# A gated attention and feed-forward kernel on one core: last batch's units moved, two blocks' turns exchanged, Down products made transposed

## The chip, the core and the metric

The kernel runs on one NeuronCore of one Trainium2 chip. The metric is device time in microseconds; the kernel before has a median of 1188.56 us over 12 runs (1186.95 to 1189.96). PE is TensorE (matmuls), PEld its weight load, DVE is VectorE, ACT is ScalarE, POOL is GpSimd and SP is SyncE, which here only issues DMAs. `Lnnn` is a line of the kernel before.

## The reference

```python
scores = (1.0 / S) * np.matmul(z, z.transpose(0, 2, 1))   # z: 8 x 3008 x 64
attn = np.maximum(scores, 0.0) ** 2
x = (u * np.matmul(attn, v)).reshape(B * S, D)            # u, v: 8 x 3008 x 256
h = x @ w_in                                              # 256 x 2048
g = h * (1.0 / (1.0 + np.exp(-1.702 * h)))
out = g @ w_out                                           # 2048 x 256, float32 out
```

Scores are symmetric, so a block of squared scores can be computed once and turned for the other triangle.

## The kernel before

**Chunks.** Each batch's 3008 rows are cut into six chunks of 512 (the last 448); rows are also counted in 24 blocks of 128, the last of which has 64 rows and is stored twice, in both halves of the partitions. A *unit* (i, jp) is a pair of row blocks of scores against chunk i: PE makes the scores (L235), ACT applies Relu into a tile `rl` (L256), DVE squares it into a tile `a` (L270, L261). Units on or above the diagonal only are computed; those of other chunks are turned by a DMA transpose from SP into tiles `tt` (`turn_unit`, L298), halves of a diagonal pair into `ad` (L263), and the last chunk's own unit into `al` (L277).

**Attention.** `attend` runs over the 24 row blocks of V as weights with squared scores moving (L358), the sum over blocks in PSUM; most matmuls use half of the array's rows in pairs. In batches after the first, chunk i reads its own first blocks, then those behind the diagonal, then turned blocks of earlier chunks, and at the end the three blocks of the last chunk, which come from `tt` too. `gate` (L375) multiplies with `u`, which arrives in column groups of 32 and is turned by a 32 x 32 transpose on DVE (L202). Scores of later units are put between the attention's steps by tables: `SCHED` says before which step of which chunk how many units are taken from the queue. `SCHED_LAST` is the table of the last batch. The first two units of a batch that are still missing are taken behind the last product of the batch before.

**Feed-forward.** `up_group` (L399) multiplies with W1 for two of 16 blocks of 128 features, ACT applies Gelu (L407), and a second pass, on DVE (L411) or on ACT (L409) for some groups, scales into `gt`. The Down projection pairs neighbouring row blocks, columns and feature halves in a seven-product scheme (P1 to P7, Winograd's form of Strassen): `left_sum` forms S1 to S4 on DVE (L467 to L476), `weight_sums` four sums of W2 once. Each product is 8 matmuls per pair of row blocks; P6, P7 and P4 add to P1's bank, P3 to P5's. Between them ACT copies banks out and DVE adds (L530, L532, L536). Batches come in twos: the two halves of the last row block of an even and an odd batch are joined, so an even batch's last block has 384 rows (one pair and an `odd` block, L493), an odd one's 512.

**Order.** The order of all instructions on each engine is the program's order, with a manual schedule: there is no planner. From group 16 on, an up group and a product alternate; ten or so products remain at the end of a batch, and with the last one the store of the last block. Stores (`store`, L562) go out on SP, with the last 64 rows of two batches on POOL; in the last batch's last block `store_part` (L551 to L556) issues quarters on SP and ACT. All DMAs of SP go out in order, and each also waits for the one issued eight DMAs earlier. `y` tiles have two buffers; they share these with the `zst` tiles of the next z.

**First batch.** Its squared blocks are turned in the order of the list `ORDER0`, each pair as soon as both units are there and all earlier entries are done.

Of the kernel before, what the change touches and what calls it, by code (L numbers as in the profile page):

```python
# [9 lines left out]
F32 = mybir.dt.float32  # L10
F16 = mybir.dt.float16
P = 128
# [3 lines left out]
def kernel(  # L16
# [13 lines left out]
    AF = mybir.ActivationFunctionType  # L30
    ALU = mybir.AluOpType

    B, S, D = u.shape
# [26 lines left out]
    W2 = const.tile([P, NFF, D], F16, name="W2")  # L60
    WT = const.tile([P, 4, NFF // 2, P], F16, name="WT")
# [180 lines left out]
    def square(b, i, jp, sc):  # L242
# [35 lines left out]
        if jp // 2 > i and (turned(b, i) or jp < NU - 2):  # L278
            if b and i == 0 and LATE:
                late.append(((jp + 2) % NU, lambda: turn_unit(b, i, jp, a)))  # L280
            elif b == 0 and jp < NU - 2:
                squared.setdefault((i, jp // 2), []).append(lambda: turn_unit(b, i, jp, a))
                while ORDER0 and len(squared.get(ORDER0[0], ())) == 2:
                    for turn_it in squared.pop(ORDER0.pop(0)):
# [2 lines left out]
                turn_unit(b, i, jp, a)  # L287


    ORDER0 = [(0, 1), (0, 2), (1, 2), (0, 3), (1, 3), (0, 4), (2, 3), (1, 4), (2, 4), (3, 4)]  # L290
    squared = {}

    def turn_unit(b, i, jp, a):
# [89 lines left out]
        return [lambda k=k: step(k) for k in range(len(order))]  # L383


    GT, Y = {}, {}

    def blocks(b):

        return [(i, CH if i < NCH - 1 or b % 2 else LFULL) for i in range(NCH)]  # L390

    def up_group(b, q):
        k, fg = divmod(q, NFG)
        i, n = blocks(b)[k]
        hg = ps2.tile([P, FFG, CH], F32, name="hg", tag="ps2")
        for e in range(FFG):
            ff = fg * FFG + e
            for c in range(NCC):
                pe.matmul(  # L399
                    hg[:, e, :n], W1[:, c, ff * P:(ff + 1) * P], XT[b, i][:, c, :n],  # L400
                    start=(c == 0), stop=(c == NCC - 1),
                )
        if fg % 2 == 0:
            GT[b, k, fg // 2] = pa.tile([P, CB, CH], F16, name="gt", tag="tt", bufs=14)
        g = GT[b, k, fg // 2][:, (fg % 2) * FFG:(fg % 2 + 1) * FFG, :n]
        gf = pw.tile([P, FFG, CH], F32, name="gf", tag="gf")
        act.activation(gf[:, :, :n], hg[:, :, :n], AF.Gelu_apprx_sigmoid, scale=1.0 / FSC)  # L407
        if q >= LAGY and q % 4 == 1:
            act.activation(g, gf[:, :, :n], AF.Copy, scale=FSC)  # L409
        else:  # L410
            dve.tensor_scalar(g, gf[:, :, :n], FSC, None, ALU.mult)  # L411
        for s_ in [SUMS.pop(0) for _ in range(min(len(SUMS), 1 + (len(SUMS) > 8)))]:
            s_()
        if fg in (NFG - 3, NFG - 1):
            SUMS.extend(left_sums(b, k, fg == NFG - 1))
# [9 lines left out]

    SUMS, ST = [], {}
    LO, HI = slice(0, NFF // 2), slice(NFF // 2, NFF)
    C0, C1 = slice(0, P), slice(P, D)

    def load_w(k):  # L430

# [8 lines left out]
            pool.dma_start(W2[:, fs], moe_w_out.rearrange("(fo p) c -> p fo c", p=P)[:, fs])  # L440

    def weight_sums():
        b11, b12, b21, b22 = W2[:, LO, C0], W2[:, LO, C1], W2[:, HI, C0], W2[:, HI, C1]
# [44 lines left out]
    def odd_block(b, k):  # L488

        s = blocks(b)[k][1] // P - 1  # L490
        yp = ps1.tile([P, D], F32, name="yp", tag="ps1")
        for ff in range(NFF):
            pe.matmul(  # L493
                yp, GT[b, k, ff // CB][:, ff % CB, s * P:(s + 1) * P], W2[:, ff, :],
                start=ff == 0, stop=ff == NFF - 1,
            )
        act.activation(Y[b, k][:, s, :], yp, AF.Copy, scale=1.0 / FSC)

    def product(b, k, name):
        if name == "odd":  # L500
            odd_block(b, k)
            return
        mm = pairs(b, k)
        right = {
            "P1": W2[:, LO, C0], "P2": W2[:, HI, C0], "P3": W2[:, HI, C1], "P4": WT[:, 3],
            "P5": WT[:, 0], "P6": WT[:, 1], "P7": WT[:, 2],
        }[name]
        if name in ("P1", "P2", "P5"):
            ST[b, k, "bank" + name] = ps1.tile([P, 2, P], F32, name="st", tag="ps1")
        bank = ST[b, k, "bank" + {"P6": "P1", "P7": "P1", "P4": "P1", "P3": "P5"}.get(name, name)]  # L510
        for m in range(mm):
            for ff in range(NFF // 2):
                h, f = divmod(ff, CB)
                lhs = {
                    "P1": lambda: left(b, k, h, 0), "P2": lambda: left(b, k, h + 2, 0),
                    "P4": lambda: left(b, k, h + 2, 1),
                }.get(name) or (lambda: ST[b, k, {"P3": "S4", "P5": "S1", "P6": "S2", "P7": "S3"}[name], h])
                pe.matmul(  # L518
                    bank[:, m, :], lhs()[:, f, m, :], right[:, ff, :],
                    start=name in ("P1", "P2", "P5") and m == 0 and ff == 0,  # L520
                    stop=ff == NFF // 2 - 1, skip_group_check=True,
                )
        if name == "P1":
            Y[b, k] = pw.tile([P, CB, D], F32, name="y", tag="y")
        y = Y[b, k].rearrange("p (m o) c -> p m o c", o=2)[:, :mm]
        bank = bank[:, :mm]
        if name in ("P1", "P6", "P7"):
            u_ = pw.tile([P, 2, P], F32, name="u" + name, tag="u" + name, bufs=1 + (name != "P1"))
            u_ = ST[b, k, "after" + name] = u_[:, :mm]
            act.activation(u_, bank, AF.Copy, scale=1.0 / FSC)  # L530
        if name == "P4":
            act.activation(y[:, :, 1, C0], bank, AF.Copy, scale=1.0 / FSC)  # L532
        outs = {"P2": (0, C0, "P2", "P1"), "P7": (1, C1, "P5", "P7"), "P3": (0, C1, "P5", "P6")}
        if name in outs:
            o, c, x, u_ = outs[name]
            dve.scalar_tensor_tensor(  # L536
                y[:, :, o, c], ST[b, k, "bank" + x][:, :mm], 1.0 / FSC, ST[b, k, "after" + u_], ALU.mult, ALU.add,
            )
        if b == B - 1 and k == NCH - 1:
            if name in ("P2", "P7", "P4", "P3"):  # L540
                store_part(b, k, *{"P4": (1, C0)}.get(name) or outs[name][:2])
        elif name == "P3":
            store(b, k, sp)

    def store_part(b, k, o, c):

        r0 = b * S + k * CH
        y = Y[b, k].rearrange("p (m o) c -> p m o c", o=2)[:, :, o, c]
        if o == 0:
            dst = out[r0:r0 + 3 * P].rearrange("(s t) c -> t s c", t=P)[:, ::2, c]  # L550
            sp.dma_start(dst, y)  # L551
            return
        sp.dma_start(out[r0 + P:r0 + 2 * P, c], y[:, 0])
        for h in range(2):
            r1 = (b - h) * S + S0
            act.dma_start(out[r1:r1 + SREM, c], y[h * SREM:(h + 1) * SREM, 1])  # L556

    def store(b, k, eng):
        i, n = blocks(b)[k]
        r0 = b * S + i * CH  # L560
        full = min(n, S - i * CH) // P
        eng.dma_start(out[r0:r0 + full * P].rearrange("(n p) c -> p n c", p=P), Y[b, k][:, :full, :])  # L562
        if full < n // P:
            for h_, bb in enumerate((b, b - 1)):
                pool.dma_start(
                    out[bb * S + S0:(bb + 1) * S], Y[b, k][h_ * SREM:(h_ + 1) * SREM, full, :],
                )


    LAGY = 2 * NFG  # L570
    HEAD = 2

    def pieces(b, i):
# [74 lines left out]
    for b in range(B):  # L648
# [95 lines left out]
```

## Time and profile before

| | |
|---|---|
| median of 12 runs | 1188.56 us |
| profiled execution, own time | 1188.99 us |
| its span, first to last instruction | 1187.1 us |
| mean granted clock of TensorE | 0.998 |
| PE busy | 1178.9 us (99%) |
| DVE, ACT busy | 838.9 us (71%), 819.8 us (69%) |
| DMA: bytes, mean rate | 142.88 MB, 120 GB/s |
| Down matmuls (L518), four groups | 5152 of 128 columns, 24% of the chain that ended last |
| output stores on SP (L562 and L551 to L553) | 51, of 64 to 512 KB |
| transposes of u on DVE (L202) | 48, mean 1213 ns |

The span is what the profile covers; the device time of the same execution is 1.9 us longer. The page's chain follows the work that ended last back through what released each step, so a share of the chain is time on the path. Busy time of PE overlaps itself (a matmul's record holds its whole pipeline), so the pace of matmuls is read from the chain's pieces, as time divided by count. A row of the timeline has start, length, engine, line, operation, tiles and count; what stands in brackets is how long the engine idled before, and for what. `SPq` rows are DMA issues, and last as long as the issue.

### The profile page before, as it was taken

The page shows a single profiled execution, that of the slowest core. Times are in us where ns is not written, and L with a number is a line of the kernel's source. Part 1 is how long each engine was busy: PE and PEld are TensorE (multiplying, and loading weights), DVE is VectorE, ACT ScalarE, POOL GpSimd, SP SyncE. Part 2 cuts the span into 40 slices and gives each one's busy share as a digit, 9 for nine tenths or more (in the row PEclk, how much of TensorE's full clock was granted, in tenths as well). Part 3 has the DMA queues.
Part 4 walks back from the last instruction along what each step waited for, and adds up shares of the span by engine and source line. Part 5 has one row for each costly group of instructions (what it writes and reads, how often), then busy time and mean ns, then how long its engine had stood idle before and what let it go on. Part 6 is the DMA issues. An engine that isn't in the chain of part 4 may idle for free.

```text
span 1187.1 us, 27918 instructions
## 1 busy us (share of the span) xinstructions
PE 1178.9 (99%) x11526; PEld 699.4 (59%) x11526; DVE 838.9 (71%) x1441; ACT 819.8 (69%) x997; POOL 228.4 (19%) x319
## 2 busy tenths in 40 slices
PE   9999999999999999999999999999999999999998
PEld 3446764467644675447754478445784457744577
DVE  6788865777758776587765877658776587763776
ACT  7878874688647876478764787757867578661785
POOL 5233101231012310142001420024100251001000
PEclk9999999999999999999999999999999999999999
DMA  9997667666786687955789556895559865693012
GB/s 221 185 128 127 134 145 136 75 107 141 140 139 75 108 161 144 129 82 93 148 152 128 89 101 150 156 110 98 115 118 166 114 98 107 137 168 77 1 37 73
DMA packets 378880, 142.88 MB, mean 120 GB/s; under 512 B 320032, under 2 KB 372640, under 8 KB 378752
## 3 DMA queue, kind: packets, MB, share of 16 engines
q1 hardware_dynamic: 320464, 99.39, 45.8%
q0 software_dynamic: 56768, 40.39, 22.7%
q8 instruction: 90, 1.47, 0.5%
q10 hardware_dynamic: 1520, 1.31, 0.3%
q14 instruction: 38, 0.31, 0.1%
HBM read 60.29 MB, written 24.64 MB: 72 GB/s over the span
## 4 chain that ended last, share of the span: by engine, by line
PE 97%; ACT 1%; DVE 1%; issue 0%; DMA 0%; SPq 0%; DVEq 0%; ACTq 0%
PE o L358 39%; PE hg L399 27%; PE st L518 24%; PE sc L235 6%; ACT rl L256 1%; PE yp L493 1%; DMA al<-a 0%; PE w L99 0%; ACT ZT L143 0%; DVE a L270 0%; SPq L277 0%; DVE ut L202 0%; ACT gf L407 0%; DVE WT L446 0%; DVE WT L447 0%
## 5 line engine op out<-in xcount | busy, mean ns | idle before, releaser
L407 ACT ACTIVATE gf<-hg 128x1024 f32<-128x1024 f32 (+1 forms) x384 | 385.9, 1005 | 146.0 <-PE hg L399 121.5
L256 ACT ACTIVATE rl<-sc 128x1024 f16<-128x1024 f32 (+1 forms) x301 | 287.6, 993 | 150.9 <-PE sc L235 105.7
L358 PEld LDWEIGHTS <-V 64*128 64x128 f16 (+1 forms) x4052 | 217.4, 94 | 257.4 <-issue 13.2
L399 PE MATMUL hg<-xt,W 128*128 128x512 f16 (+1 forms) x1408 | 355.8, 375 | 0.0
L411 DVE TENSOR_SCALAR gt<-gf 128x1024 f16<-128x1024 f32 (+1 forms) x320 | 223.8, 699 | 138.6 <-ACT gf L407 135.9
L358 PE MATMUL o<-a,V 64*128 64x512 f16 (+3 forms) x2240 | 296.6, 369 | 0.3 <-DVE a L270 0.3
L270 DVE TENSOR_TENSOR a<-rl 128x1024 f16<-128x1024 f16 (+1 forms) x266 | 178.4, 674 | 120.4 <-ACT rl L256 119.2
L195 POOL DMA_DIRECT2D uq<-in_u_dram x188 | 127.8, 687 | 689.7 <-PE sc L235 455.6
L358 PE MATMUL o<-tt,V 64*128 64x512 f16 (+1 forms) x1510 | 232.0, 377 | 0.0
L399 PEld LDWEIGHTS <-W 128*128 128x128 f16 x1536 | 139.4, 98 | 120.1 <-issue 3.9
L518 PEld LDWEIGHTS <-gt 128*128 128x128 f16 x2944 | 177.1, 98 | 32.2
L518 PEld LDWEIGHTS <-s 128*128 128x128 f16 x2208 | 133.7, 98 | 25.6 <-issue 0.4
L235 PE MATMUL sc<-ZT 64*128 64x512 f16 (+3 forms) x688 | 114.5, 356 | 0.6 <-ACT ZT L143 0.3
L518 PE MATMUL st<-WT,gt 128*128 128x128 f16 x1472 | 97.8, 219 | 0.0
L518 PE MATMUL st<-WT,s 128*128 128x128 f16 x1472 | 96.5, 219 | 0.2 <-ACT uP L530 0.2
L518 PE MATMUL st<-W,gt 128*128 128x128 f16 x1472 | 96.5, 219 | 0.0
L536 DVE SCALAR_TENSOR_TENSOR y<-st,uP 128x256 f32<-128x256 f32 (+1 forms) x144 | 57.6, 407 | 28.4 <-ACT uP L530 19.9
L530 ACT ACTIVATE uP<-st 128x256 f32<-128x256 f32 (+1 forms) x144 | 53.1, 368 | 31.4 <-DVE y L536 16.2
L375 DVE TENSOR_TENSOR xt<-o,ut 128x512 f16<-128x512 f32 x80 | 51.3, 682 | 27.6 <-PE o L358 27.6
L409 ACT ACTIVATE gt<-gf 128x1024 f16<-128x1024 f32 (+1 forms) x64 | 66.0, 1031 | 2.1
L474 DVE TENSOR_TENSOR s<-s,gt 128x1024 f16<-128x1024 f16 (+1 forms) x96 | 64.3, 670 | 1.1
L472 DVE TENSOR_TENSOR s<-gt 128x1024 f16<-128x1024 f16 (+1 forms) x96 | 64.0, 667 | 0.0
(53 smaller groups left out, 602.6 us busy)
## 6 DMA issues: line engine op xcount, KB each, us to landing
out_dram<-y SPq DMA_DIRECT2D x40, 512.0 KB, 3.5
uq<-in_u_dram POOLq DMA_DIRECT2D x156, 128.0 KB, 3.6
V<-in_v_dram POOLq DMA_DIRECT2D x35, 256.0 KB, 6.4
tt<-a SPq DMA_TRANSPOSE x232, 3.7
uq<-in_u_dram POOLq DMA_DIRECT2D x32, 112.0 KB, 4.8
out_dram<-y SPq DMA_DIRECT2D x7, 384.0 KB, 3.0
vst<-in_v_dram SPq DMA_DIRECT2D x3, 512.0 KB, 5.7
zst<-in_z_dram POOLq DMA_DIRECT2D x7, 192.0 KB, 8.9
```

The costliest lines, as they stand in the source:

```text
L195: eng.dma_start(uq[k * QW:(k + 1) * QW, :n // QW].rearrange("t q c k -> t q (c k)"), src[:, :, cs])
L235: pe.matmul(sc[:, r, :q1 - q0], zt[h, 2 * kp + r, :], zt[h].rearrange("d n p -> d (n p)")[:, q0:q1], start=True, stop=True,)
L256: act.activation(rl[:, :, :n], sc[:, :, :n], AF.Relu, scale=csc)
L270: dve.tensor_tensor(a[:, :, :n], rl[:, :, :n], rl[:, :, :n], ALU.mult)
L358: ins = pe.matmul(acc[c][:, :n], V16[b][h, j].rearrange("p (c k) -> p k c", k=NCC)[:, c], weights(b, i, j)[h], start=(k, m) == first[c], s ...
L399: pe.matmul(hg[:, e, :n], W1[:, c, ff * P:(ff + 1) * P], XT[b, i][:, c, :n], start=(c == 0), stop=(c == NCC - 1),)
L407: act.activation(gf[:, :, :n], hg[:, :, :n], AF.Gelu_apprx_sigmoid, scale=1.0 / FSC)
L409: act.activation(g, gf[:, :, :n], AF.Copy, scale=FSC)
L411: dve.tensor_scalar(g, gf[:, :, :n], FSC, None, ALU.mult)
L472: dve.tensor_tensor(s_, a21, a22, ALU.add)
L474: dve.tensor_tensor(s_, ST[b, k, "S1", h], a11, ALU.subtract)
L518: pe.matmul(bank[:, m, :], lhs()[:, f, m, :], right[:, ff, :], start=name in ("P1", "P2", "P5") and m == 0 and ff == 0, stop=ff == NFF // ...
```

## The change

There are three parts.

- `SCHED_LAST`: in the last batch, the two units of the last chunk itself are taken before step 2 of chunk 4 instead of step 24.
- `ORDER0`: in the first batch the blocks of chunk 2 for chunk 3 are turned before those of chunk 0 for chunk 4.
- The Down projection makes its products transposed. The weights (W2 by even and odd columns, `W2K`, or their sums) are the stationary operand and two row blocks of `gt` or S move together, so that a pair is one matmul of 256 columns instead of two of 128; for the odd block, 32 of 128 instead of 16 of 256. Output channels then lie on partitions. ACT copies P1, P6, P7 and P4 straight into `y`, and DVE adds in place. `store` turns `y` into the single-buffered tile `yo` by a 32 x 32 transpose on DVE, and stores it in four column groups of 32 partitions, pieces of 256 bytes, all on SP. An odd batch's last block is stored in twelve DMAs, the last batch's last block in two steps on SP, ACT and POOL. Of the scaling passes, groups 1, 3 and 5 of every eight go to ACT instead of 1 and 5.

```diff
-    ORDER0 = [(0, 1), (0, 2), (1, 2), (0, 3), (1, 3), (0, 4), (2, 3), (1, 4), (2, 4), (3, 4)]
+    ORDER0 = [(0, 1), (0, 2), (1, 2), (0, 3), (1, 3), (2, 3), (0, 4), (1, 4), (2, 4), (3, 4)]
...
-        if q >= LAGY and q % 4 == 1:
+        if q >= LAGY and q % 8 in (1, 3, 5):
             act.activation(g, gf[:, :, :n], AF.Copy, scale=FSC)
...
+    W2K = W2.rearrange("p f (c k) -> p f k c", k=NCC)
...
-        for ff in range(NFF):
-            pe.matmul(
-                yp, GT[b, k, ff // CB][:, ff % CB, s * P:(s + 1) * P], W2[:, ff, :],
-                start=ff == 0, stop=ff == NFF - 1,
-            )
-        act.activation(Y[b, k][:, s, :], yp, AF.Copy, scale=1.0 / FSC)
+        for c in range(NCC):
+            for ff in range(NFF):
+                pe.matmul(
+                    yp[:, c, :], W2K[:, ff, c], GT[b, k, ff // CB][:, ff % CB, s * P:(s + 1) * P],
+                    start=c == 0 and ff == 0, stop=ff == NFF - 1, skip_group_check=True,
+                )
+        act.activation(Y[b, k][:, :, s * P:(s + 1) * P], yp, AF.Copy, scale=1.0 / FSC)
...
-        for m in range(mm):
-            for ff in range(NFF // 2):
...
-                pe.matmul(
-                    bank[:, m, :], lhs()[:, f, m, :], right[:, ff, :],
...
+        for ff in range(NFF // 2):
...
+            pe.matmul(
+                bank, right[:, ff], lhs()[:, f],
+                start=name in ("P1", "P2", "P5") and ff == 0, stop=ff == NFF // 2 - 1, skip_group_check=True,
+            )
         if name == "P1":
-            Y[b, k] = pw.tile([P, CB, D], F32, name="y", tag="y")
...
+            Y[b, k] = pw.tile([P, NCC, CH], F32, name="y", tag="y")
+
+        y = Y[b, k].rearrange("p k (m o t) -> p k m o t", o=2, t=P)[:, :, :mm]
+        copy = {"P1": (0, 0), "P6": (0, 1), "P7": (1, 1), "P4": (1, 0)}
+        if name in copy:
+            o, c = copy[name]
+            act.activation(y[:, c, :, o], bank, AF.Copy, scale=1.0 / FSC)
...
         if b == B - 1 and k == NCH - 1:
-            if name in ("P2", "P7", "P4", "P3"):
-                store_part(b, k, *{"P4": (1, C0)}.get(name) or outs[name][:2])
+            if name in ("P4", "P3"):
+                store(b, k, [1, 3] if name == "P4" else [0, 2])
         elif name == "P3":
-            store(b, k, sp)
+            store(b, k, range(blocks(b)[k][1] // P))
...
+    def store(b, k, ss):
+
         i, n = blocks(b)[k]
-        r0 = b * S + i * CH
...
+        r0, nq = b * S + i * CH, P // QW
+        if (b, k) not in YO:
+            YO[b, k] = pw.tile([P, CH // QW, QW, NCC], F32, name="yo", tag="yo", bufs=1)
+        yo, step = YO[b, k], ss[1] - ss[0]
+        if step == 1:
+            m = len(ss) * nq
+            dve.transpose(
+                yo[:, :m].rearrange("p q c k -> p q k c"),
+                Y[b, k][:, :, :m * QW].rearrange("p k (q t) -> p q k t", t=QW),
+            )
+        else:
+            for s_ in ss:
+                dve.transpose(
+                    yo[:, s_ * nq:(s_ + 1) * nq].rearrange("p q c k -> p q k c"),
+                    Y[b, k][:, :, s_ * P:(s_ + 1) * P].rearrange("p k (q t) -> p q k t", t=QW),
                 )
+        whole = [s_ for s_ in ss if i * CH + (s_ + 1) * P <= S]
+        for cb in range(P // QW):
+            ps, cs = slice(cb * QW, (cb + 1) * QW), slice(cb * NCC * QW, (cb + 1) * NCC * QW)
+            eng = (sp, act)[cb // 2 if len(whole) < 2 else cb % 2] if step > 1 else sp
+            rows = out[r0:r0 + (whole[-1] + 1) * P].rearrange("(q t) c -> t q c", t=QW)
+            if step == 1:
+                eng.dma_start(rows[:, :, cs], yo[ps, :len(whole) * nq].rearrange("t q c k -> t q (c k)"))
+            else:
+                for s_ in whole:
+                    (pool if len(whole) > 1 and cb == 3 else eng).dma_start(
...
+            if len(whole) < len(ss):
+                q0 = ss[-1] * nq
+                for h in range(2):
+                    r1 = (b - h) * S + S0
+                    eng.dma_start(
...
-    SCHED_LAST = SCHED | {3: {n: 1 for n in (14, 34)} | {NJ: 2}, 4: {NJ: 2}, 5: {}}
+    SCHED_LAST = SCHED | {3: {n: 1 for n in (14, 34)} | {NJ: 2}, 4: {2: 2}, 5: {}}
```

More of the change, by code (lines that the diff above doesn't have):

```diff
@@ L383, in attend @@
         return [lambda k=k: step(k) for k in range(len(order))]
-    GT, Y = {}, {}
+    GT, Y, YO = {}, {}, {}
     def blocks(b):
@@ L427 @@
     LO, HI = slice(0, NFF // 2), slice(NFF // 2, NFF)
-    C0, C1 = slice(0, P), slice(P, D)
+    W2K = W2.rearrange("p f (c k) -> p f k c", k=NCC)
     def load_w(k):
@@ L442, in weight_sums @@
     def weight_sums():
-        b11, b12, b21, b22 = W2[:, LO, C0], W2[:, LO, C1], W2[:, HI, C0], W2[:, HI, C1]
+        b11, b12, b21, b22 = W2K[:, LO, 0], W2K[:, LO, 1], W2K[:, HI, 0], W2K[:, HI, 1]
         t1, t2, t3, t4n = (WT[:, m] for m in range(4))
@@ L490, in odd_block @@
         s = blocks(b)[k][1] // P - 1
-        yp = ps1.tile([P, D], F32, name="yp", tag="ps1")
-        for ff in range(NFF):
-            pe.matmul(
-                yp, GT[b, k, ff // CB][:, ff % CB, s * P:(s + 1) * P], W2[:, ff, :],
-                start=ff == 0, stop=ff == NFF - 1,
-            )
-        act.activation(Y[b, k][:, s, :], yp, AF.Copy, scale=1.0 / FSC)
+        yp = ps1.tile([P, NCC, P], F32, name="yp", tag="ps1")
+        for c in range(NCC):
[5 more added lines that the diff above has]
+        act.activation(Y[b, k][:, :, s * P:(s + 1) * P], yp, AF.Copy, scale=1.0 / FSC)
     def product(b, k, name):
@@ L504, in product @@
         right = {
-            "P1": W2[:, LO, C0], "P2": W2[:, HI, C0], "P3": W2[:, HI, C1], "P4": WT[:, 3],
+            "P1": W2K[:, LO, 0], "P2": W2K[:, HI, 0], "P3": W2K[:, HI, 1], "P4": WT[:, 3],
             "P5": WT[:, 0], "P6": WT[:, 1], "P7": WT[:, 2],
@@ L509, in product @@
             ST[b, k, "bank" + name] = ps1.tile([P, 2, P], F32, name="st", tag="ps1")
-        bank = ST[b, k, "bank" + {"P6": "P1", "P7": "P1", "P4": "P1", "P3": "P5"}.get(name, name)]
-        for m in range(mm):
-            for ff in range(NFF // 2):
[L513 to L518, printed above, removed]
-                    bank[:, m, :], lhs()[:, f, m, :], right[:, ff, :],
-                    start=name in ("P1", "P2", "P5") and m == 0 and ff == 0,
-                    stop=ff == NFF // 2 - 1, skip_group_check=True,
-                )
@@ L523, in product @@
-        if name == "P1":
-            Y[b, k] = pw.tile([P, CB, D], F32, name="y", tag="y")
[L525 to L532, printed above, removed]
@@ L533, in product @@
-        outs = {"P2": (0, C0, "P2", "P1"), "P7": (1, C1, "P5", "P7"), "P3": (0, C1, "P5", "P6")}
+        bank = ST[b, k, "bank" + {"P6": "P1", "P7": "P1", "P4": "P1", "P3": "P5"}.get(name, name)][:, :mm]
+        for ff in range(NFF // 2):
+            h, f = divmod(ff, CB)
+            lhs = {
+                "P1": lambda: left(b, k, h, 0), "P2": lambda: left(b, k, h + 2, 0),
+                "P4": lambda: left(b, k, h + 2, 1),
+            }.get(name) or (lambda: ST[b, k, {"P3": "S4", "P5": "S1", "P6": "S2", "P7": "S3"}[name], h])
+            pe.matmul(
+                bank, right[:, ff], lhs()[:, f],
+                start=name in ("P1", "P2", "P5") and ff == 0, stop=ff == NFF // 2 - 1, skip_group_check=True,
+            )
@@ L534, in product @@
+        if name == "P1":
+            Y[b, k] = pw.tile([P, NCC, CH], F32, name="y", tag="y")
[4 more added lines that the diff above has]
+            act.activation(y[:, c, :, o], bank, AF.Copy, scale=1.0 / FSC)
+        outs = {"P2": (0, 0, "P2"), "P7": (1, 1, "P5"), "P3": (0, 1, "P5")}
         if name in outs:
-            o, c, x, u_ = outs[name]
+            o, c, x = outs[name]
@@ L536, in product @@
             dve.scalar_tensor_tensor(
-                y[:, :, o, c], ST[b, k, "bank" + x][:, :mm], 1.0 / FSC, ST[b, k, "after" + u_], ALU.mult, ALU.add,
+                y[:, c, :, o], ST[b, k, "bank" + x][:, :mm], 1.0 / FSC, y[:, c, :, o], ALU.mult, ALU.add,
             )
         if b == B - 1 and k == NCH - 1:
-            if name in ("P2", "P7", "P4", "P3"):
-                store_part(b, k, *{"P4": (1, C0)}.get(name) or outs[name][:2])
+            if name in ("P4", "P3"):
+                store(b, k, [1, 3] if name == "P4" else [0, 2])
@@ L542, in product @@
         elif name == "P3":
-            store(b, k, sp)
[L545 to L556, printed above, removed]
@@ L558, in store @@
-    def store(b, k, eng):
-        i, n = blocks(b)[k]
-        r0 = b * S + i * CH
[L561 to L566, printed above, removed]
-                )
+            store(b, k, range(blocks(b)[k][1] // P))
@@ new lines, in store @@
+    def store(b, k, ss):
+        i, n = blocks(b)[k]
+        r0, nq = b * S + i * CH, P // QW
[13 more added lines that the diff above has]
+                    Y[b, k][:, :, s_ * P:(s_ + 1) * P].rearrange("p k (q t) -> p q k t", t=QW),
+                )
+        whole = [s_ for s_ in ss if i * CH + (s_ + 1) * P <= S]
[8 more added lines that the diff above has]
+                    (pool if len(whole) > 1 and cb == 3 else eng).dma_start(
+                        rows[:, s_ * nq:(s_ + 1) * nq, cs],
+                        yo[ps, s_ * nq:(s_ + 1) * nq].rearrange("t q c k -> t q (c k)"),
+                    )
+            if len(whole) < len(ss):
[3 more added lines that the diff above has]
+                    eng.dma_start(
+                        out[r1:r1 + SREM].rearrange("(q t) c -> t q c", t=QW)[:, :, cs],
+                        yo[ps, q0 + h * nq // 2:q0 + (h + 1) * nq // 2].rearrange("t q c k -> t q (c k)"),
+                    )
```

## The prediction

> **What bounds the kernel now.** I read the totals and the chain that ended last first.
>
> ```profile
> span 1187.1 us, 27918 instructions
> ...
> PE 1178.9 (99%) x11526; PEld 699.4 (59%) x11526; DVE 838.9 (71%) x1441; ACT 819.8 (69%) x997; POOL 228.4 (19%) x319
> ...
> PE 97%; ACT 1%; DVE 1%; issue 0%; DMA 0%; SPq 0%; DVEq 0%; ACTq 0%
> ```
>
> TensorE is the bound nearly everywhere, so time goes only with matmul time, with a wait of PE, or at the two ends. The chain in order of time gives the pace of a matmul:
>
> ```profile
> 155.92 1.75 PE yp L493 x16
> ...
> 1088.05 1.18 SPq L277
> 1089.28 3.79 DMA al<-a
> ...
> 1173.19 9.84 PE st L518 x176
> ```
>
> A Down product of 128 columns takes 9.84/176 = 55.9 ns, one of 256 columns 1.75/16 = 109.4 ns. One stretch of the chain is a transfer. The timeline there:
>
> ```profile
> 1093.20 0.37 PE L358 MATMUL o<-al,V 64*128 64x448 f16 x2 [1.91 <-DMA al<-a]
> ...
> 1096.06 1.78 PE L399 MATMUL hg<-xt,W 128*128 128x512 f16 x4
> ...
> 1098.06 1.03 PE L399 MATMUL hg<-xt,W 128*128 128x512 f16 x4
> ```
>
> PE stands 1.91 us, and afterwards runs at half rate: four matmuls take 1.78 where they later take 1.03. From 1093.20 to 1097.68 pass eight hg and some five o; at the later rate (0.216 and 0.19 us each) that is 2.7 us, so the slow clock cost 1.8 more.
>
> What the rest leans on is SP's queue at a change of batch (1 to 2 here), and the end:
>
> ```profile
> 303.82 4.68 SPq L562 DMA_DIRECT2D out_dram<-y  x2
> 309.79 3.48 SPq L298 DMA_TRANSPOSE tt<-a  x2
> 313.37 1.21 SPq L263 DMA_TRANSPOSE ad<-a  x1
> 314.68 11.74 SPq L298 DMA_TRANSPOSE tt<-a  x8
> ...
> 324.93 1.67 PE L358 MATMUL o<-tt,V 64*128 64x512 f16 x14
> ```
>
> ```profile
> 1179.09 1.28 DVE L476 TENSOR_TENSOR s<-gt,s 128x1024 f16<-128x1024 f16 x2
> ...
> 1183.06 0.42 DVE L536 SCALAR_TENSOR_TENSOR y<-st,uP 128x256 f32<-128x256 f32 x1 [1.36 <-PE st L518]
> 1184.09 0.37 SPq L551 DMA_DIRECT2D out_dram<-y  x1
> ```
>
> Two stores pass, then SP issues DMA transposes without a break (one per 1.3 to 1.4 us), and PE reads them some us later.
>
> **What the Trainium skill says.** "TensorE: Matmul & The Clock Gate", section "Wait — 56ns, not 53.3ns?": warm matmuls start N/2.4 GHz plus about 2.5 ns apart, so one of 256 columns saves one such fixed cost against two of 128; the trace agrees (55.9 and 109.4). The same page, "What's actually happening": idling halves the clock; the rows at 1093 to 1097 agree. Its "Weight-path perf modes" lets fast weight load take strided columns; the strided V loads (mean 94 ns against 98 for W1) agree, but not at a 56 ns pace. "DMA: Bandwidth & Descriptors", "Specifications": under 512 B a transfer misses line rate; no 256 B store to HBM is in this trace.
>
> **The change, part by part.**
>
> *Last batch, units at slot 2 of chunk 4.* The scores, ACT, DVE and two al transposes move ahead by 22 slots of 0.216 us, 4.8 us, against a wait of 1.91. ACT idled 7.26 us before this work, and SP has only two tt transposes from 1077.79 to 1081.07, so nothing is pushed. Gain 1.91 + 1.8 = 3.7; at least 1.9 if the clock drops anyway.
>
> *First batch, order of the turns.* Two pairs of transposes change places on SP. No PE wait for tt stands there, so 0; it shows only if the displaced block (0,4) came late, and chunk 4 reads it some 18 us after its present landing.
>
> *Merged matmuls.* A batch has 5 whole blocks, an odd one a sixth: 44 blocks with 7 x 8 pairs = 2464 pairs, each 2 x 55.9 - 109.4 = 2.4 ns: -5.9. The odd block becomes 32 of 55.9 for 16 of 109.4, four times: +0.2. Sum -5.7. Bounds: -6.5, and +11 if the strided weights of the 224 products that stay at 128 columns loaded 50 ns too slowly; I take -5.7.
>
> *ACT and DVE in the Down stage.* From 270 to 298 us ACT is busy 22.6 and DVE 21.2 of 28. ACT gains a 1.03 us copy in every eighth group (16 groups there: +2.1); DVE loses two 0.70 copies and gains about 2.3 output transposes priced by L202, 1.21 us for the same 1024 elements: +1.4. Both stay under 25, so PE, two PSUM buffers ahead, hides them: 0. The copies of P1, P6 and P7 go into y instead of a buffer of their own, same number and size; the four weight sums now read every second element, at worst 0.7 us more each, once, in chunk 5 of the first batch, under DVE's idle 29%: 0. If that cover went, each late us would be a PE us.
>
> *Change of batch.* Here the new waits bite. `yo` has one buffer: the transposition of block 5 waits on DVE until block 4's four stores have landed, and next batch's squares queue behind it. After an odd batch, in the times of before: block 4's last sum ends at 303.76, its transposition at 304.97; four stores issue. Stores of this shape cost as the four uq loads on SP at the start: 2.17 us for four, 0.54 each. The last goes out at 306.65 and lands about 2.9 later (that of the 512 KB store at 303.82): 309.6. Meanwhile S4, which followed at 303.67, ends at 306.25, the sum of P7 at 306.7, whose bank P3 needs at 306.55: PE waits 0.2. Transposition of block 5: 309.6 to 310.8. The squares end at 311.5 and 312.2 instead of 309.72 and 310.63; PE reads them at about 311.6 and 312.0: 0 to 0.3. ACT has three rl buffers and can go on for three units behind them.
>
> SP then issues twelve stores (four column groups; whole rows and two half blocks), where before it issued one and POOL two: 310.8 + 12 x 0.54 = 317.3. The transposes that began at 309.79 begin there. The fifth and sixth tt (units (1,10) and (1,11)), issued at 317.4 and 318.8, come after four others and one ad: the sixth starts at 317.3 + 5 x 1.36 + 1.3 = 325.4 and lands 3.3 later (median of the tt issues there), 328.7. PE wants it at 325.6 (four steps of 0.216 and two scores after the first o<-tt at 324.50): a stall of 3.1. Three such changes (into batches 2, 4, 6): 9.3, less 0.1 each that PE is late already: 9.0. Each idles PE longer than the 1.91 us that halved the clock; I put 1.2 on each (0 to 2): 3.6. With the bank wait, 0.6, together +13.2.
>
> After an even batch there are only four stores and half-size sums: transposition at 447.8 to 449.0, landing 453.6, block 5's (768 elements, 0.9) to 454.5, stores to 456.7 against a first transpose at 453.96: 2.7 late, and the same read (469.8 against a landing at 465.4) leaves 4.3. 0, with 1.6 to spare.
>
> *The end.* Block 4's sum ends at 1179.17, its transposition 1180.4, stores issued to 1182.6, landed 1184.9. Only then go the two 256-element transpositions of P4's half (0.37 each by L202's ratio) to 1185.6, then the sum of P3 and two more, to 1186.8. From 1185.6 SP issues six stores, then four: 10 x 0.54 = 1191.0; the last lands 2 us after its start and the span closes 0.4 later (as 1184.09, +2.6, 1187.1 now): about 1193. +6.0; bounds +3.5 (0.35 us an issue) and +8.
>
> **Sum.** 1187.1 - 3.7 - 5.7 + 13.2 + 6.0 = 1196.9 of span. The profiled run itself took 1188.99, 1.9 more, and the median of 1188.56 lies 0.4 under that: 1198.4, say 1198.
>
> **Rivals.** *The queue absorbs the stores.* The stall falls away if the stores end on SP by about 314: with 310.8 as their start, 0.27 us an issue, or an earlier landing. For: every out store on SP cost only 0.37, and transposes waited up to 0.9 us there for nothing that need remain. Against: 32- and 64-partition DMAs on SP cost 0.47 to 0.6 at the start. Then 1187.1 - 3.7 - 5.7 + 5.5 + 0.6 = 1183.8, 1185 as median: faster. A stall of 1 us without a slow clock would give 1188: the same.
>
> *Narrow stores are slow.* 256 B pieces cost as much as 1 KB ones: block 4's stores take 6 us, not 2, the wait for `yo` grows by 3 at all seven changes and at the end: 3 x 3 + 3 x 2 + 3 more, about 1215. Against: the four uq loads with 256 B pieces landed in 3.4 us in full traffic.
>
> *ACT becomes the bound* in the Down stage: copies in groups 1, 3, 5 in a row need 3.8 us in a spell of 3.5; with 12 copies a batch 12 x 0.3 x 8 = 29 us more is the very most. Against: groups 6 to 8 have none, and PE leads by more than 1 us.
>
> **How the numbers follow.** Stall at the odd changes, 1192 to 1206: 0.57. Absorbed, 1183 to 1187.5: 0.21. In between: 0.07. Slow narrow stores or ACT, over 1206: 0.15. The range of 8 in 10 is 1184 to 1210; the likeliest alone has 1192 to 1206. Faster by over 0.2% (about what this measurement can tell) 0.21, within 0.07, slower 0.72.
>
> **What would show it.** The merged st matmuls at 109 ns and none but the partial block's at 56; no PE wait at al in the last batch; SP's row of stores before the tt row at each change, tt starting some 7 us later after odd batches and 3 after even ones; a PE wait named "DMA tt<-a" near chunk 1's end in batches 2, 4 and 6 with half-rate matmuls behind it; DVE idle on stores before block 5's transposition; 6 us more between the last matmul and the end. I am wrong if no such PE wait stands there, or if PE waits on ACT inside the Down stage.

## The result, and the profile after

The changed kernel took 1210.75 us (median of 8 runs, 1208.06 to 1213.88) against 1188.03 of the kernel before (32 runs): ratio 1.019, 95% interval 1.0179 to 1.0202. That is 22.7 us slower, where 10 were forecast; the direction was right, and the time lies just above the range.

Totals of the profiled execution (its own time 1208.06), from the page:

```profile
span 1206.3 us, 23332 instructions
...
PE 1178.7 (98%) x9126; PEld 680.2 (56%) x9126; DVE 872.1 (72%) x1460; ACT 846.1 (70%) x1029; POOL 221.5 (18%) x315
```

The span grew by 19.2 us (from 1187.1). PE runs 2400 matmuls fewer, and yet its busy time is that of before (1178.9). What merging saved is filled by matmuls at half rate and by the starts of waits, which still lie under the records of the matmuls ahead; the rest of the waits comes on top. The list of what PE waited for (total us, times, longest) shows three names of which only the first was forecast:

```profile
PE o L358 <- DMA tt<-a: 8.6, 3, 3.1
PE o L358 <- DVE a L270: 4.7, 5, 1.2
PE hg L399 <- ACT rl L256: 2.0, 1, 2.0
```

**Forecast and there: SP's queue at the change from batch 1 to 2.** The timeline (start, duration, engine, line; in brackets the idle time ahead and what ended it):

```profile
307.00 7.44 SPq L567 DMA_DIRECT2D out_dram<-yo  x5
...
312.85 1.25 DVE L551 STREAM_TRANSPOSE yo<-y 128x1024 f32<-128x1024 f32 x1 [2.83 <-ACT rl L256]
...
318.85 0.94 SPq L578 DMA_DIRECT2D out_dram<-yo  x2
319.89 2.61 SPq L298 DMA_TRANSPOSE tt<-a  x2
...
332.21 1.04 PE L358 MATMUL o<-tt,V 64*128 64x512 f16 x8 [3.10 <-DMA tt<-a]
```

Block 4's stores go out from 307.00, the transposition of block 5 begins only at 312.85, twelve stores follow until 319.8, and the row of tt transposes that began at 309.79 before begins at 319.89. PE stands 3.10 us, at the step that the prediction named. The bracket at 312.85 names ACT, but L551 reads nothing of ACT's rl there; the second-buffer experiment below shows what it waited for.

**Not forecast: the squares behind that transposition.** After batch 0:

```profile
162.12 0.29 DVE L533 SCALAR_TENSOR_TENSOR y<-st,y 128x128 f32<-128x128 f32 x1 [0.62 <-PE st L518]
165.14 0.98 DVE L551 STREAM_TRANSPOSE yo<-y 128x768 f32<-128x768 f32 x1 [2.73 <-DMA out_dram<-yo]
166.04 1.25 DVE L270 TENSOR_TENSOR a<-rl 128x1024 f16<-128x1024 f16 x2
...
166.75 1.00 PE L358 MATMUL o<-a,V 64*128 64x512 f16 x6 [0.56 <-DVE a L270]
```

DVE has its sum at 162.41 and stands 2.73 us until block 4's stores have landed in full; the next batch's squares queue behind, and PE waits for them. The four stores issued from 159.60 on took 3.9 us (median, 4.1 at most) to land, those at the change from 1 to 2 up to 4.4. Before, the one 512 KB store at 303.82 landed in 2.9 us.

**Not forecast: the weight sums.** Before:

```profile
97.01 0.68 DVE L449 TENSOR_TENSOR WT<-W,WT 128x1024 f16<-128x1024 f16 x1
...
98.48 1.02 ACT L256 ACTIVATE rl<-sc 128x1024 f16<-128x1024 f32 x1 [0.93 <-DVE a L273]
```

After:

```profile
95.17 1.22 DVE L446 TENSOR_TENSOR WT<-W 128x1024 f16<-128x1024 f16 x1
...
98.70 1.22 DVE L449 TENSOR_TENSOR WT<-W,WT 128x1024 f16<-128x1024 f16 x1
...
100.70 1.02 ACT L256 ACTIVATE rl<-sc 128x1024 f16<-128x1024 f32 x1 [3.06 <-DVE a L273]
...
101.77 1.02 PE L399 MATMUL hg<-xt,W 128*128 128x512 f16 x4 [2.01 <-ACT rl L256]
```

Each sum takes 1.22 us where one took 0.68 before (683 ns). The squares queued behind the four sums end late, so ACT, which needs their rl buffer, waits 3.06 us and not 0.93, and PE waits for ACT to empty a PSUM buffer for hg.

**The end.** After the last st matmuls:

```profile
1195.66 1.03 PE L518 MATMUL st<-s,W 128*128 128x256 f16 x8
...
1198.71 0.77 DVE L557 STREAM_TRANSPOSE yo<-y 128x256 f32<-128x256 f32 x2 [2.77 <-DMA out_dram<-yo]
...
1202.06 0.87 ACTq L570 DMA_DIRECT2D out_dram<-yo  x2
```

PE ends at 1196.7, the span at 1206.3: 9.6 us, where before 4.1 lay between (1183.0 to 1187.1).

### The profile page after: what moved, and what is told of

The parts are those of the page before. It is cut to its first block, busy times and chain, and to the rows that moved or that the text cites. A ratio compares the mean times of both kernels' runs of the same rounds, so it can differ in the third digit from the quotient of the medians.

```text
span 1206.3 us, 23332 instructions
## 1 busy us (share of the span) xinstructions
PE 1178.7 (98%) x9126; PEld 680.2 (56%) x9126; DVE 872.1 (72%) x1460; ACT 846.1 (70%) x1029; POOL 221.5 (18%) x315
## 5 line engine op out<-in xcount | busy, mean ns | idle before, releaser
L411 DVE TENSOR_SCALAR gt<-gf 128x1024 f16<-128x1024 f32 (+1 forms) x288 | 199.9, 694 | 114.7 <-ACT gf L407 114.1
L399 PEld LDWEIGHTS <-W 128*128 128x128 f16 x1536 | 149.7, 98 | 127.3 <-issue 5.1
L518 PEld LDWEIGHTS <-WT 128*128 128x128 f16 x1536 | 145.4, 98 | 46.8 <-issue 0.4
L518 PEld LDWEIGHTS <-W 128*128 128x128 f16 x1152 | 109.3, 98 | 34.2 <-issue 1.3
L409 ACT ACTIVATE gt<-gf 128x1024 f16<-128x1024 f32 (+1 forms) x96 | 98.9, 1030 | 3.0
L518 PE MATMUL st<-gt,WT 128*128 128x256 f16 (+1 forms) x768 | 96.1, 268 | 0.0
L529 ACT ACTIVATE y<-st 128x256 f32<-128x256 f32 x192 | 70.6, 368 | 35.6 <-PE st L518 35.0
L518 PE MATMUL st<-s,WT 128*128 128x256 f16 (+1 forms) x768 | 94.8, 268 | 0.2 <-ACT y L529 0.2
L518 PE MATMUL st<-gt,W 128*128 128x256 f16 (+1 forms) x768 | 94.8, 268 | 0.0
L551 DVE STREAM_TRANSPOSE yo<-y 128x1024 f32<-128x1024 f32 (+1 forms) x47 | 58.0, 1234 | 22.6 <-DMA out_dram<-yo 17.9
L533 DVE SCALAR_TENSOR_TENSOR y<-st,y 128x256 f32<-128x256 f32 (+1 forms) x144 | 57.2, 406 | 14.1 <-issue 5.8
```

What stands on the lines that cost most here:

```text
L399: pe.matmul(hg[:, e, :n], W1[:, c, ff * P:(ff + 1) * P], XT[b, i][:, c, :n], start=(c == 0), stop=(c == NCC - 1),)
L518: pe.matmul(bank, right[:, ff], lhs()[:, f], start=name in ("P1", "P2", "P5") and ff == 0, stop=ff == NFF // 2 - 1, skip_group_check=True,)
L529: act.activation(y[:, c, :, o], bank, AF.Copy, scale=1.0 / FSC)
```

## The experiments

The theory is the prediction's account, with the two waits just seen added. Medians are compared, with the interval of the ratio to the kernel before. That kernel measured 1187.71 alongside runs 1 to 4, 1187.72 alongside 5 to 8 and 1188.57 alongside 9 to 12, so a difference between runs of different groups can be off by some 0.9 us.

**1. The last batch's edit alone**, on the kernel before.

```diff
-    SCHED_LAST = SCHED | {3: {n: 1 for n in (14, 34)} | {NJ: 2}, 4: {NJ: 2}, 5: {}}
+    SCHED_LAST = SCHED | {3: {n: 1 for n in (14, 34)} | {NJ: 2}, 4: {2: 2}, 5: {}}
```

> The kernel before, with the last batch's edit alone (chunk 5's own units at slot 2 of chunk 4). Theory: the 1.91 us wait for al and the half-rate stretch behind it go, worth 3.5 to 3.7 us as in the trace of after: 1184.4 against 1188.0. Rival, the clock falls later for another reason: only the wait goes, 1186.1. Rival, the wait only moves: 1188.

Measured 1185.43 against 1187.71 (ratio 0.9969, 0.9956 to 0.9982): 2.3 us. Its timeline has neither the wait for al nor the slow stretch:

```profile
1093.24 0.35 PE L358 MATMUL o<-al,V 64*128 64x448 f16 x2
1093.53 0.36 PE L358 MATMUL o<-a,V 128*128 128x448 f16 x1
1093.73 1.03 PE L399 MATMUL hg<-xt,W 128*128 128x512 f16 x4
```

By the traces the stretch is some 3.5 us shorter; by the medians 2.3, inside the bounds of the prediction. The traced execution happens to have a wait of 1.7 us for W1 in the first batch that the one of before hasn't, which hides part of it in the spans (1185.1 and 1187.1).

**2. A second buffer for yo.**

```diff
-            YO[b, k] = pw.tile([P, CH // QW, QW, NCC], F32, name="yo", tag="yo", bufs=1)
+            YO[b, k] = pw.tile([P, CH // QW, QW, NCC], F32, name="yo",
+                               **({"tag": "gf"} if k == NCH - 1 else {"tag": "yo", "bufs": 1}))
```

> The changed kernel, with a second buffer for yo: block 5's transposition takes the Gelu buffer (tag gf, free by then), so it doesn't wait for block 4's stores. Theory (the single buffer delays squares and SP alike): the waits of PE on DVE a L270 at all seven changes go (3.7 us after even batches, 2.7 after odd ones), SP starts the twelve stores some 2.4 us sooner, so the three stalls at tt fall from 3.0 to about 0.6 and less clock is lost: 3.7 + 2.7 + 7.2 + 1 to 3 us, about 1195 against 1210.8. Rival, the number of stores on SP decides by itself: only the 6.4 of the squares go and the stalls keep 2.5 us or more, about 1204. Rival, DVE is late for its load and not for yo: 1210, nothing goes.

Measured 1198.43 (ratio 1.0077, 1.0054 to 1.0100), 12.3 us less than the changed kernel. The waits on squares are gone from the list, those on tt are not:

```profile
PE o L358 <- DMA tt<-a: 6.2, 3, 2.2
PE hg L399 <- ACT rl L256: 2.0, 1, 2.0
```

So the transposition waited for yo, squares and SP's start behind it. But the theory's 0.6 a stall was too low: 2.1 each remain, near the rival's 2.5. The number of stores decides most of the stall by itself.

**3. The half-block stores on POOL.**

```diff
-                    eng.dma_start(
+                    (pool if step == 1 else eng).dma_start(
                         out[r1:r1 + SREM].rearrange("(q t) c -> t q c", t=QW)[:, :, cs],
```

> The changed kernel, with the eight 16 KB stores of the two half blocks issued by POOL (4 stores on SP at an odd change, as at an even one). Theory (SP's queue): the three tt stalls of 3.0 us go, 9.1 us, with the half-rate stretches behind them, 2 to 3.5; the waits on the squares, 6.4, stay: about 1198.5. Rival, the late start behind yo decides and not the number: stalls stay at 2 us or more, 1207. Rival, POOL's own queue is held by the stores and u or z comes late: new PE waits, 1210 or more.

Measured 1199.49 (ratio 1.0082, 1.0059 to 1.0104), 11.3 less, as expected. The list is the complement of the one above:

```profile
PE o L358 <- DVE a L270: 4.8, 6, 1.1
...
PE o L358 <- DMA tt<-a: 1.2, 3, 0.6
```

Eight issues of some 0.45 us on SP made the stalls; the wait on the squares has nothing to do with them.

**4. The weight sums apart.**

```diff
-                if (b, i, n) == (0, NCH - 1, NJ + 4):
-                    for sum_ in weight_sums():
-                        sum_()
+                if b == 0 and i == NCH - 1 and n in (17, NJ + 4):
+                    wsums = wsums if n > NJ else weight_sums()
+                    wsums.pop(0)()
...
             product(b, *prods.pop(0))
+            if b == 0 and q in (head, head + 2):
+                wsums.pop(0)()
```

> The changed kernel, with the four weight sums taken apart: the first at step 17 of chunk 5 in the first batch, the second at step 28, the third and fourth behind the first and third products of the Down stage, instead of all four at step 28. Theory: four sums of 1.22 us in a row hold the squares up and give the 2.0 us wait of PE on ACT rl L256 there, so it goes: 1208.6 against 1210.8. Rival, DVE has no room in that stretch: the wait moves to another place, 1210 to 1211. Rival, PE reaches the sums sooner than they are made: slower, over 1211.

Measured 1209.88 (five runs, 1205.62 to 1210.86; ratio 1.0162, 1.0138 to 1.0185). The wait on ACT rl is gone from the trace; the time alone doesn't decide, since its interval touches that of the changed kernel. The traced execution, the slowest of the five, has a wait of 3.4 us for W1 in the first batch, which the changed kernel's trace hasn't. Run 10 repeats the question where the rest is quiet.

**5. The three repairs together**: edits 2, 3 and 4.

> The changed kernel with the three repairs together: yo of block 5 in the Gelu buffer, half-block stores on POOL, weight sums taken apart. Theory (three separate causes, which add up): from the 1199.5 of the kernel with the half stores on POOL go the waits on squares (4.8 us and 0.8 of small follow-ons), what is left at tt (1.2), the sums' 2.0, and 1 us at the end, where the transposition of block 5 no longer waits for yo: 1188 to 1190, so about as fast as before (1187.7) in spite of the end. Rival, the repairs overlap (each cures the same lateness): 1194 or more. Rival, there is a further cost inside the Down stage that none of them touches: 1191 to 1194.

Measured 1187.77 (ratio 0.9992, 0.9978 to 1.0007): 23.0 us less than the changed kernel, level with before. PE has no wait left over 0.2 us after the first chunks. The single gains (12.3 and 11.3, and 3.7 for the sums by run 10) add to more than 23.0, since the yo buffer also shortens the stalls that the POOL stores take away. The 1 us expected at the end didn't come: from PE's last matmul to the end of the span are 11.4 us in this trace (1174.1 to 1185.5), 1.8 more than in the changed kernel.

**6. The merged products taken apart again**, on the three repairs.

```diff
-            pe.matmul(
-                bank, right[:, ff], lhs()[:, f],
+            for m in range(mm):
+                pe.matmul(
+                    bank[:, m], right[:, ff], lhs()[:, f, m],
```

> As the kernel with three repairs, but with the merged products taken apart again: two matmuls of 128 columns with the same weights in place of one of 256, transposed as in the change. Theory: 2464 pairs x 2.4 ns = 5.9 us slower than the three repairs. Rival, the saving is smaller since the waits at the ends of products (0.31 us for a bank, four times) take it back: 4 to 5. Rival, the strided weights set the pace of a 128-column product (not 56 but 60 ns or more): over 10 us slower.

Measured 1193.47 (ratio 1.0043, 1.0030 to 1.0057): 5.7 us slower than with them merged, near the 5.9 of the pairs and equal to the prediction's sum for this part. In the trace of this run the 128-column products start 55 to 56 ns apart, as before, so weights read in steps of two cost nothing at this pace.

**7. The Gelu's second pass shared as before** (`q % 4 == 1` for `q % 8 in (1, 3, 5)`), on the three repairs.

> As the kernel with three repairs, but with the Gelu's second pass shared between ACT and DVE as before (ACT in two of eight groups, not three). Theory: both engines are hidden in the Down stage: within 0.5 us of the three repairs. Rival, ACT bounds the Down stage: faster by 1 us or more. Rival, DVE, with its transpositions, needs that relief: slower by 1 us or more.

Measured 1187.93 (ratio 0.9999, 0.9985 to 1.0013), 0.2 from 1187.77: neither ACT nor DVE bounds the Down stage.

**8. The end: the last block not transposed**, on the three repairs.

```diff
+            if (b, k) == (B - 1, NCH - 1):
+                for m in range(mm):
+                    pe.matmul(
+                        bank[:, m], lhs()[:, f, m], right[:, ff],
...
+                continue
...
+        if (b, k) == (B - 1, NCH - 1):
+            y = Y[b, k].rearrange("p k f -> p (k f)").rearrange("p (m o t k) -> p k m o t", o=2, t=P, k=NCC)
```

> As the kernel with three repairs, and in the last block of the last batch the products not transposed (two of 128 columns for one of 256, as before), so that its rows go straight from y to the output in whole rows, with no DVE transposition: five stores for twenty. Theory: the end after the last matmul falls from some 8.5 us to the 4.1 of before or 0.5 more, against 0.1 us for 56 unmerged pairs: 4 to 4.5 us less than the three repairs, about 1184. Rival, the 256 B pieces and not the number of stores and the transpositions were slow at the end: also 4, and the stores' own landing times tell it. Rival, writes of every second column into y slow ACT and DVE: 1186 or more.

Measured 1184.34 (ratio 0.9968, 0.9959 to 0.9977), 3.4 less, somewhat under the expectation; its end takes 7.2 us for 11.4. But the timeline of its end shows a wait that the edit itself made:

```profile
1181.00 0.43 DVE L543 SCALAR_TENSOR_TENSOR y<-st,y 128x256 f32<-128x256 f32 x1 [4.15 <-DMA out_dram<-y]
```

Even and odd rows shared one tile; the last sum, which writes the even rows, stood until the odd rows' stores had read it.

**9. Tiles of their own for even and odd rows**, and two of block 4's last four stores on POOL.

```diff
+            YO["end"] = [pw.tile([P, 2, D], F32, name="ye", tag="y"), pw.tile([P, 2, D], F32, name="yu", tag="gf")]
...
-            eng = (sp, act)[cb // 2 if len(whole) < 2 else cb % 2] if step > 1 else sp
+            eng = pool if (b, k) == (B - 1, NCH - 2) and cb % 2 else sp
```

> As the kernel with three repairs and the untransposed last block, but the even and the odd rows of that block in tiles of their own (there DVE's last sum waited 4.15 us for the odd rows' stores to have read the shared y), and two of the four stores of block 4 in the last batch on POOL. Theory: that wait was all that kept the end at 12 us; it falls to some 8, and the time to 1180 to 1181, which is also 1187.7 less the 2.3 of the last batch's edit and 5.7 of merging, plus about 1 for the end. Rival, landing of the last stores itself takes the time: 1183.5 or more.

Measured 1181.82 (ratio 0.9943, 0.9930 to 0.9956): 6.8 us faster than the kernel before, and the fastest here. The last sum now waits for nothing but its matmuls:

```profile
1174.43 0.42 DVE L547 SCALAR_TENSOR_TENSOR ye<-st,ye 128x256 f32<-128x256 f32 x1 [0.83 <-PE st L520]
```

Against the three repairs this is 5.95 us: what the transposed end cost there, where it took 11.4 us and now takes 5.1 (1174.4 to 1179.5). The two edits weren't measured apart.

**10. The weight sums in a row again**, on run 9 (edit 4 undone).

> As the kernel with own tiles for the last block, and the four weight sums in a row at step 28 again. Theory: PE waits 2.0 us at ACT rl L256 in the first batch, as in the changed kernel's trace: slower by 2.0 to 2.2 us than with the sums apart. Rival, the trace's wait is repaid later in the batch: within 0.5 us (with the sums apart and nothing else mended, the medians differed by 0.9 only).

Measured 1185.49 (17 runs; ratio 0.9976, 0.9968 to 0.9985), 3.7 us slower. The wait is back in its timeline:

```profile
101.69 1.02 PE L399 MATMUL hg<-xt,W 128*128 128x512 f16 x4 [2.02 <-ACT rl L256]
```

The spans differ by 2.5 (1182.0 and 1179.5), the medians by 1.2 more. Lost clock fits this. Ten of the 17 executions have a granted clock of 0.997 or 0.998 and took 1185.3 to 1187.5 us; the seven at 0.999 or 1.0 took 1183.7 to 1185.5. And the trace of run 12, where the sums are in a row too, has half rate behind the same wait:

```profile
102.92 1.78 PE L399 MATMUL hg<-xt,W 128*128 128x512 f16 x4 [2.01 <-ACT rl L256]
```

These four matmuls take 1.78 us, here and in the changed kernel 1.02. That this happens often enough to make up the 1.2 us is not shown.

**11. The first batch's order of turns as before**, on run 9.

> As the kernel with own tiles for the last block, and the first batch's order of turns as before (blocks (0,4) in front of (2,3)). Theory: nobody waits for those transposes in either order: within 0.3 us. Rival, chunk 3 reads (2,3) before it has landed: slower by 1 to 2 us. Rival, (0,4) comes late in the new order: faster by 1 us.

Measured 1181.88 (ratio 0.9945, 0.9931 to 0.9958): 0.1 from 1181.82, so nothing, as the prediction had it.

**12. Keeping PE busy through the stalls**, on the changed kernel.

```diff
+                if b in (2, 4, 6) and (i, n) == (1, 20):
+                    w = ps1.tile([P, CH], F32, name="w", tag="ps1")
+                    for m in range(12):
+                        pe.matmul(w, ident, W1[:, 0, :CH], start=m == 0, stop=m == 11)
```

> The changed kernel, with 12 idle matmuls of 512 columns (2.6 us at full rate, result not used) in front of step 20 of chunk 1 in batches 2, 4 and 6, where PE stands 2.75 to 3.3 us for tt. Theory (idling there costs clock besides the wait): PE waits only 0.2 to 0.7 there, no half-rate stretch follows, and the time falls by 2 to 4 us, to about 1207 to 1209 against 1210.8. Rival, the clock falls for other reasons (a drop that comes anyway): 1210.8, no change. Rival, the clock doesn't fall and all of the three stalls is waiting: 1210.8 too, and no half-rate stretch in either trace.

Measured 1203.89 (ratio 1.0129, 1.0111 to 1.0146): 6.9 us less, for 36 matmuls more. In the changed kernel, at the change from batch 3 to 4:

```profile
627.62 1.89 PE L358 MATMUL o<-tt,V 64*128 64x512 f16 x8 [2.90 <-DMA tt<-a]
629.30 1.06 PE L235 MATMUL sc<-ZT 64*128 64x512 f16 x4
```

With the idle matmuls:

```profile
626.31 2.76 PE L686 MATMUL w<-W,ident 128*128 128x512 f16 x12
629.16 1.04 PE L358 MATMUL o<-tt,V 64*128 64x512 f16 x8
630.03 0.60 PE L235 MATMUL sc<-ZT 64*128 64x512 f16 x4
```

The stall takes as long, but eight o matmuls behind it take 1.04 us and not 1.89: idling had cost clock. Not all of the 6.9 is that. The waits on squares also fell, from 4.7 us to 1.9 (mostly into batches 4, 5 and 7), for a reason that no run settles; 4.1 remain for the clock, against an expected 2 to 4. The granted clock agrees: its median over the executions is 0.993 in the changed kernel and 0.997 here.

## Why the prediction was right or wrong

| step | predicted | shown, by medians | by which run |
|---|---|---|---|
| last batch's units | -3.7 (at least -1.9) | -2.3 | 1 |
| merged matmuls | -5.7 | -5.7 | 6 |
| first batch's order | 0 | -0.1 | 11 |
| ACT and DVE in the Down stage (share of the Gelu) | 0 | -0.2 | 7 |
| weight sums | 0 | +3.7 | 10 |
| changes of batch | +13.2 | +21.1 (23.0 of the repairs, less 3.7, and 1.8 by which they made the end longer) | 5, 10 |
| the end | +6.0 | +5.5 (9.6 for 4.1 us, by the traces) | before, after |

The shown terms sum to +22.0 of the +22.7; 0.7 is assigned to nothing, less than groups of runs differ by.

The traces alone give the same picture. From matmul start to matmul start, after and run 5 differ by 22.6 us up to PE's last matmul: 9.2 at tt, 6.9 at the squares of the seven changes, 2.5 behind the weight sums, 3.1 in matmuls at half rate behind two of the stalls, 0.9 in small pieces.

*Merging, the end, the order, the Down stage.* These steps held to within half a us. That run 9 gives 6.0 for the end is a coincidence: it took away an end that run 5 had made longer. The wait for a bank before P3, put at 0.2, is 0.31 (its first matmul starts 0.42 us behind the one ahead, others 0.11), at the three odd changes and once more at the end. Run 6 doesn't have it, so the 5.7 is net of it. In the Down stage, from 272 to 300 us, DVE is busy 23.83 and ACT 24.65 of 28: under the 25 of the prediction.

*The last batch.* The place and kind of the gain are right. The term of 1.8 for the slow clock was read from one execution and is not that large in the median.

*The stalls at tt.* Place and cause are right, and the size too: 9.0 predicted, 8.6 in the list. SP's row started at 318.0 in the times of before (319.89, less the 1.87 us by which block 4's last sum ended later: 305.63 for 303.76), predicted 317.3; twelve stores took some 0.47 us each, not 0.54, which made up for part of a later beginning. The size is luck in part: the data came some 1.6 us later than predicted (330.3 for 328.7), but PE, held up at the squares, asked about as much later.

*The step that failed* is the landing of block 4's stores, "lands about 2.9 later", and with it the cover given to the squares. The 2.9 was that of one 512 KB store in 1 KB pieces. The last of the four stores in 256 B pieces landed 4.4 us after its issue at the change from 1 to 2, and the four from 159.60 on took up to 4.1. It was not other traffic, since both stretches moved little but these 0.52 MB; before (303 to 308 us) and after (307 to 313 us):

```profile
q1 hardware_dynamic: 528, 0.52, 30.5%
```

```profile
q1 hardware_dynamic: 2112, 0.52, 48.9%
```

The columns are packets, MB and share of 16 engines' time. A packet thus took an engine 46 ns before (0.305 x 5 us x 16 / 528) and 22 ns after (0.489 x 6 us x 16 / 2112), with a quarter of the bytes: the same data kept the engines busy about twice as long. No run tells the shorter pieces from the 32 partitions that such a store reads. For tt this hardly mattered. For the squares, given "0 to 0.3" after odd batches and only the tt slack ("0, with 1.6 to spare") after even ones, it was all: the prediction's own times put their end at 311.5 against a read at 311.6, so each late us of a landing is a PE us. After even batches the squares weren't asked about at all. Together this is 4.7 us of listed waits, 6.9 from matmul to matmul, against 0 to 0.9.

*The slow clock* was 3.6 in the prediction, is 3.1 in the trace of after and about 4 by run 12; this term is right, though spread differently: none behind the 3.10 us stall in batch 2, where eight matmuls take 1.04 us, and 0.85 us and more in batch 4. The Trainium skill, "TensorE: Matmul & The Clock Gate", section "What's actually happening", says that the window in which activity is counted runs freely and isn't tied to the kernel, so where a stall falls in it can decide; that fits a drop at one stall and not at its twin, and medians that differ from one profile, but no run here shows the window itself.

*The weight sums.* Here a price was right and a cover wrong. "At worst 0.7 us more each" became 0.54 (1.22 for 0.68). The Trainium skill, "VectorE: DVE Perf Modes", section "What auto-detection actually checks", says that two 16-bit sources are worked at the double rate only where every tensor has step 1, which these lost; the trace agrees. But "under DVE's idle 29%: 0" took an average for a place: in the trace of before ACT already waited 0.93 us for a square queued behind the sums, and 4 x 0.54 = 2.16 us of lateness arrived at PE as 2.0. The prediction named the price of a lost cover and then didn't look at the rows between 95 and 104 us.

*The rivals.* The queue didn't absorb the stores: 0.47 us an issue, where 0.27 was needed. ACT is no bound (run 7). Slow narrow stores were right in kind and too strong in size: a 256 B piece cost half of a 1 KB one, not as much. (That rival's sum, 3 x 3 + 3 x 2, also prices six changes and not the seven that it names.) What carried the result above the range was neither, but two waits on DVE's queue that had been costed at 0.

## What to carry to other kernels

When a new instruction on an in-order engine waits for a transfer, list all that is queued behind it, with the time at which each is read, and price the landing for the pieces that are stored; a slack of 0.1 us is no cover. An engine's mean idle share covers nothing either: look at the rows around the place, above all if the operand's step changes an operation's rate. Where a merged operation gains a few us, the layout that it forces must be paid for with a second buffer, few DMA issues on the queue that feeds the bound engine, and an end of its own; with these, the same change is 0.6% faster instead of 1.9% slower.

## What the runs showed of the hardware that was not expected

- Twelve idle matmuls (2.76 us) in front of each of three stalls made the whole kernel 6.9 us faster (some 2.8 of it by shorter waits elsewhere), with the stalls unchanged; after two stalls of about 3 us in the same kernel, matmuls ran at full rate once (1.04 us for eight) and at about half once (1.89).
- A wait of PE cost more in the medians than in the trace: 3.7 us for one of 2.0 (run 10). Behind this same wait four matmuls took 1.02 us in one trace and 1.78 in another.
- Stores of 128 KB in 256 B pieces landed in 2.9 us in the median over the kernel, but in up to 4.4 at a change of batch, with hardly any other traffic there. A piece of 256 B took a DMA engine 22 ns, one of 1 KB 46.
